# Three-layer kernel on one core: the weights' low words shifted by ScalarE, VectorE's conversion in one pass, and the last block stored in another order

## The chip, the core and the metric

The kernel runs on 1 core of a Trainium2 chip. The metric is the device time of one execution in microseconds. The kernel before takes 1051.12 us (median of 3 runs, 1050.27 to 1051.77). Names of engines: PE is TensorE's matmul, PEld its weight load, DVE is VectorE, ACT is ScalarE, POOL is GpSimd, SP is SyncE, which issues all DMAs here.

## The reference

Three steps follow one another. Tokens are 2304 = 4 x 576, the model width is 512.

```
attention(q, k, v)          # (4, 8, 576, 64): softmax over 4x pooled keys, repeated 4 times,
                            # plus softmax over a band |i - j| < 4
x  = attention as (2304, 512)
h  = x @ w_in               # 512 -> 2048
x  = (max(h, 0) + alpha * min(h, 0)) @ w_out          # 2048 -> 512
xn = x / sqrt(mean(x*x) + 1e-6) * rms_g
g  = xn @ w_gate            # 512 -> 1536
y  = (g * sigmoid(g) * (xn @ w_val)) @ w_out2         # 1536 -> 512
```

All inputs are 64-bit floats in DRAM, and the output is 32-bit.

## The kernel before

**Conversion of the weights.** Every weight matrix comes as pairs of 32-bit words, and the kernel makes 32-bit floats of them itself. A matrix is cut into pieces (`Piece`, L976): w_in and w_out six each, w_gate, w_val and the second w_out four each. A piece is loaded in two halves (`load`, L985) into a raw tile `wr` of 128 x 768 pairs (two halves per matrix of the first layer have 128 x 256). `decode` (L1014) works on one half with three instructions: ACT scales the high words in place (L1018), DVE shifts them left by three into the result `wc` (L1020), and DVE shifts the low words right by 29 and ORs them in (L1021). Then ACT squares the piece with a running sum (L1031), TensorE sums over the partitions (`allps`, L319), DVE makes a power of two from it, and `split` (L344) writes the weight as two 16-bit halves, high by ACT (L345) and low by DVE (L346). So a product of two matrices takes three 16-bit matmuls.

**Blocks.** The tokens are taken in 6 blocks of 384. Layer one (`m1`) runs over 16 units of 128 hidden columns: 12 matmuls `hps` (L1248), ACT and DVE for the leaky relu (L1252, L1254) and the split, and 12 matmuls `acc` (L1261) two units later. Layer two (`m2`, L1327) runs over 12 units: 24 matmuls `gps` (L1340) for gate and value, ACT's tanh (L1349), two passes of DVE (L1351, L1354), the split into `uhl` (L1356, L1357), and 9 matmuls `oacc` (L1365) two units later. At the end of a block three groups of 128 tokens are moved out of PSUM by ACT (L1395) and stored (L1407). Attention of later blocks (`local_tasks`, L431: products on DVE and POOL, L447 and L495, sums on DVE, L458 and L508) and the conversion of layer two's weights run as background work beside the matmuls of layer one's first blocks and layer two's first block.

**What sets the order.** All instructions are recorded first, then `issue_order` (L24) puts them in a fixed order on each engine. It plays the program through with a table of costs per instruction (`cost`, L86) and waits per pair of engines, 20 times back and forth, and keeps the best order. Every engine, SP included, works through its list in order, so one waiting instruction holds up all behind it. A change of a few instructions gives other costs and so another order everywhere.

**The end.** The last block's stores have a DRAM side of 4 rows of time steps by 32 chunks by 512 columns (L1405); the earliest block, in the first batch, has one of 128 rows by 512 columns (L1403).

## Time and profile before

| | |
|---|---|
| median of 3 runs | 1051.12 us |
| the profiled execution, its own time | 1050.03 us |
| its span, first to last instruction | 1048.3 us |
| mean granted TensorE clock (1 is 2.4 GHz) | 0.985 |
| PE busy | 972.9 us |
| DVE busy | 710.8 us |
| ACT busy | 474.0 us |

The profile is of one execution. Busy time is a union of an engine's instructions; a group's row gives how many instructions of one line there are, their busy time together and the mean of one, and behind the second bar the idle time of the engine just ahead of them with what ended it. The chain of waits is followed back from the last instruction. A wait's row names who waited and for whom, the total, the number of times and the longest.

### The profile page before, as it was taken

The numbers are of one execution on the slowest core, as the hardware profiler recorded it, in microseconds if no ns is written. First come the engines' busy times: TensorE is split into PE (matmuls) and PEld (weight loads), VectorE is DVE, ScalarE is ACT, GpSimd is POOL, SyncE is SP. The second block draws the span as 40 slices with busy tenths as digits, with TensorE's granted clock in tenths as the row PEclk, the third lists the DMA queues.
The fourth block names the chain that finished last, engine by engine and source line by source line (L and its number), as shares of the span: only waits on it lengthen the run. The fifth ranks groups of instructions, "written<-read, shape, count | busy, mean of one in ns | idle before, by whom it ended". The sixth has DMA issues, their size and how long they took to land.

```text
span 1048.3 us, 16289 instructions
## 1 busy us (share of the span) xinstructions
PE 972.9 (93%) x6232; PEld 610.5 (58%) x6232; DVE 710.8 (68%) x1515; ACT 474.0 (45%) x1178; POOL 141.3 (13%) x118
## 2 busy tenths in 40 slices
PE   3598998899999699999999999999999999999995
PEld 2465666668975355555666565555556566555553
DVE  0468988999999986999966599993333353442331
ACT  2896868767965365123366432222232332321211
POOL 2522121101021101333200232310000000000000
PEclk9999989999999899999999999999999999999998
DMA  9974635564322023112122021100010000000000
GB/s 169 187 162 126 189 123 159 183 195 127 116 91 91 29 92 123 48 74 61 41 74 78 22 76 46 31 21 11 1 31 2 1 1 1 1 1 8 23 1 31
DMA packets 49972, 74.54 MB, mean 71 GB/s; under 512 B 17682, under 2 KB 30886, under 8 KB 49894
## 3 DMA queue, kind: packets, MB, share of 16 engines
q1 hardware_dynamic: 49894, 73.50, 25.0%
q8 instruction: 49, 0.80, 0.3%
q14 instruction: 29, 0.24, 0.1%
HBM read 68.76 MB, written 4.72 MB: 70 GB/s over the span
## 4 chain that ended last, share of the span: by engine, by line
PE 63%; DVE 19%; DMA 7%; ACT 5%; issue 3%; SPq 1%; POOL 0%; ACTq 0%; POOLq 0%; DVEq 0%
PE gps L1340 19%; PE acc L1261 14%; PE hps L1248 13%; PE oacc L1365 9%; DMA out_dram<-ob 4%; DVE prod L508 2%; DVE ls L458 2%; DVE prod L447 1%; PE avps L649 1%; DVE w L346 1%; DVE prod L495 1%; DVE wc L1021 1%; PE lsps L837 1%; DVE hps L1254 1%; DVE lo L508 1%
## 5 line engine op out<-in xcount | busy, mean ns | idle before, releaser
L1248 PE MATMUL hps<-xt,wi 128*128 128x192 f16 (+1 forms) x1536 | 345.5, 292 | 5.7 <-DVE ghl L346 3.4
L1340 PE MATMUL gps<-x,w 128*128 128x384 f16 x1728 | 343.8, 327 | 4.1 <-DVE th L1351 2.8
L1261 PE MATMUL acc<-ghl,wo 128*128 128x384 f16 (+1 forms) x960 | 247.3, 310 | 0.4 <-ACT ob L1395 0.4
L1340 PEld LDWEIGHTS <-w 128*128 128x128 f16 x1728 | 169.8, 99 | 119.5 <-issue 8.2
L1365 PE MATMUL oacc<-w,uhl 128*128 128x512 f16 x648 | 195.1, 379 | 2.1 <-ACT ob L1395 1.7
L1248 PEld LDWEIGHTS <-wi 128*128 128x128 f16 x1536 | 148.1, 100 | 64.3 <-issue 12.9
L1261 PEld LDWEIGHTS <-wo 128*128 128x128 f16 x1344 | 129.1, 99 | 68.6 <-issue 5.8
L1254 DVE SCALAR_TENSOR_TENSOR hps<-g,oma,hps 128x192 f32<-128x192 f32 (+1 forms) x128 | 65.9, 516 | 77.9 <-ACT g L1252 77.6
L1349 ACT ACTIVATE th<-gps,tsc 128x384 f32<-128x384 f32 x72 | 41.8, 580 | 141.6 <-PE gps L1340 141.3
L1351 DVE SCALAR_TENSOR_TENSOR th<-th,gps 128x384 f32<-128x384 f32 x72 | 39.5, 549 | 97.7 <-ACT th L1349 97.6
L1365 PEld LDWEIGHTS <-uhl 128*128 128x128 f16 x648 | 63.5, 98 | 69.8 <-issue 3.2
L1252 ACT ACTIVATE g<-hps 128x384 f32<-128x384 f32 x96 | 47.0, 490 | 107.3 <-PE hps L1248 106.8
L1356 ACT ACTIVATE uhl<-gps 128x384 f16<-128x384 f32 x72 | 35.3, 490 | 111.0 <-DVE gps L1354 99.6
L447 POOL TENSOR_TENSOR prod<-cq,ckv 128x896 f32<-128x896 f32 x24 | 51.0, 2124 | 240.1 <-PE avps L649 72.6
L1261 PE MATMUL acc<-g,wo 128*128 128x384 f16 (+1 forms) x384 | 67.4, 286 | 2.3 <-DVE wo L346 1.4
L495 POOL TENSOR_TENSOR prod<-ls,ckv 128x896 f32<-128x896 f32 x24 | 44.1, 1837 | 185.0 <-DVE lo L508 97.2
L508 DVE TENSOR_TENSOR prod<-prod 128x384 f32<-128x384 f32 (+1 forms) x108 | 63.3, 596 | 2.3 <-POOL prod L495 2.3
L345 ACT ACTIVATE ghl<-hps,sc 128x384 f16<-128x384 f32 x72 | 41.8, 582 | 50.2 <-DVE hps L1254 44.3
L346 DVE SCALAR_TENSOR_TENSOR ghl<-hps,sc,ghl 128x384 f16<-128x384 f32 x72 | 44.1, 614 | 23.6 <-ACT ghl L345 23.3
L458 DVE TENSOR_REDUCE ls<-prod 128x14 f32<-128x896 f32 x54 | 57.7, 1075 | 0.0
L1357 DVE TENSOR_TENSOR uhl<-gps,uhl 128x384 f16<-128x384 f32 x72 | 39.7, 552 | 22.3 <-ACT uhl L1356 22.2
L1354 DVE SCALAR_TENSOR_TENSOR gps<-th,kap,gps 128x384 f32<-128x384 f32 x60 | 37.1, 618 | 10.6 <-PE gps L1340 7.5
(229 smaller groups left out, 1213.2 us busy)
## 6 DMA issues: line engine op xcount, KB each, us to landing
wr<-in_moe_w_out_dram SPq DMA_DIRECT2D x18, 512.0 KB
wr<-in_moe_w_in_dram SPq DMA_DIRECT2D x20, 384.0 KB
wr<-in_moe_w_gate_dram SPq DMA_DIRECT2D x8, 768.0 KB
wr<-in_moe_w_val_dram SPq DMA_DIRECT2D x8, 768.0 KB
ckv<-in_k_dram SPq DMA_DIRECT2D x7, 768.0 KB
ckv<-in_v_dram SPq DMA_DIRECT2D x7, 768.0 KB
wr<-in_moe_w_out_dram SPq DMA_DIRECT2D x20, 256.0 KB
out_dram<-ob SPq DMA_DIRECT2D x13, 256.0 KB
```

The lines of the kernel that those rows point to most:

```text
L345: nc.scalar.activation(out=hi, in_=src, func=AF.Copy, scale=s)
L346: nc.vector.scalar_tensor_tensor(out=lo, in0=src, scalar=s, in1=hi, op0=ALU.mult, op1=ALU.subtract)
L447: engs[i].tensor_tensor(out=pr, in0=view(st["q"][:, j, t:t + TP], [[D, TP], [0, ND], [1, D]]), in1=view(st["k"][:, j, t:t + TP], [[D, TP], ...
L458: nc.vector.tensor_reduce(out=st["s"][:, j, t:t + TP], in_=st.pop(("p", i)), axis=AX.X, op=ALU.add)
L495: engs[i].tensor_tensor(out=pr, in0=view(st["s"][:, j, t:t + TP], [[ND, TP], [1, ND], [0, D]]), in1=view(st["v"][:, j, t:t + TP], [[D, TP] ...
L508: add = lambda o, a, c: nc.vector.tensor_tensor(out=o, in0=a, in1=c, op=ALU.add)
L1248: nc.tensor.matmul(ps[:, j], wi[:, f + j, a, kk * 128:(kk + 1) * 128], x[:, b_, kk, c0:c0 + n], start=(i == 0), stop=(i == 3 * KK - 1))
L1252: nc.scalar.activation(out=g, in_=ps, func=AF.Relu, scale=-1.0)
L1254: nc.vector.scalar_tensor_tensor(out=ps[:, j], in0=g[:, j], scalar=oma[:, f + j:f + j + 1], in1=ps[:, j], op0=ALU.mult, op1=ALU.add)
L1261: nc.tensor.matmul(acc[e], wo_f(f)[:, a, e * 128:(e + 1) * 128], hl[:, b_], start=(f == 0 and i == 0), stop=(f == NF - 1 and i == 2))
L1340: nc.tensor.matmul(ps, w2_t[i0 + f // 3].rearrange("p a (k c) -> p a k c", k=KK)[:, a, kk, (f % 3) * 128:(f % 3 + 1) * 128], xh[:, b_, kk] ...
L1365: nc.tensor.matmul(acc[tt], t[:, a, tt * 128:(tt + 1) * 128], w[:, b_, f % 3], start=(f in first and i == 0), stop=(f in last and i == 2))
```

## The change

The conversion of all matrices but w_in is altered: ACT takes a second pass, on the low words, as an unsigned number times 2^-29, less a little over one half, through Relu, into an integer (which leaves the top three bits); DVE then shifts the high words and ORs in ACT's result in one pass. A constant column `nhalf` is added. In the last block of layer two, the `uhl` tiles are written with the tokens in another order; the last two units' `oacc` matmuls are recorded group by group; each group of 128 tokens leaves PSUM in two halves of 256 columns, one by ACT and one by DVE; and its store has a DRAM side of 32 chunks by 4 rows by 512 columns.

```diff
--- before.py
+++ after.py
@@ -289,6 +289,7 @@
 
     ident = const.tile([128, 128], F32, name="ident")
     ones = const.tile([128, 1], F32, name="ones")
+    nhalf = const.tile([128, 1], F32, name="nhalf")
     maskp = const.tile([128, 2, W, ND], F32, name="maskp")
     edge = const.tile([128, 3], F32, name="edge")
     pidx = edge[:, 2:3].bitcast(I32)
@@ -351,6 +352,7 @@
             out=ident, in_=ident, pattern=[[-1, 128]], compare_op=ALU.is_equal, fill=0.0, base=0, channel_multiplier=1
         )
         nc.vector.memset(ones, 1.0)
+        nc.vector.memset(nhalf, -0.5 - 2.0 ** -20)
         nc.gpsimd.iota(pidx, pattern=[[0, 1]], base=0, channel_multiplier=1)
         nc.vector.tensor_scalar(out=pidx, in0=pidx, scalar1=NC - 1, scalar2=None, op0=ALU.bitwise_and)
         nc.vector.tensor_scalar(out=edge[:, 0:1], in0=pidx, scalar1=0, scalar2=NEG, op0=ALU.is_equal, op1=ALU.mult)
@@ -1017,6 +1019,12 @@
             hi, lo = r[:, :, :, 1], r[:, :, :, 0]
             nc.scalar.activation(out=hi.bitcast(F32), in_=hi.bitcast(F32), func=AF.Prelu, scale=2.0 ** -112,
                                  alpha=2.0 ** 32)
+            if self.w is not w_in:
+                nc.scalar.activation(out=lo, in_=lo.bitcast(mybir.dt.uint32), func=AF.Relu, scale=2.0 ** -29,
+                                     bias=nhalf)
+                nc.vector.scalar_tensor_tensor(out=d, in0=hi, scalar=3, in1=lo,
+                                               op0=ALU.logical_shift_left, op1=ALU.bitwise_or)
+                return
             nc.vector.tensor_scalar(out=d, in0=hi, scalar1=3, scalar2=None, op0=ALU.logical_shift_left)
             nc.vector.scalar_tensor_tensor(out=d, in0=lo, scalar=29, in1=d,
                                            op0=ALU.logical_shift_right, op1=ALU.bitwise_or)
@@ -1353,8 +1361,12 @@
             kp = 2.0 ** -P_U if m == 0 else kap[:, f // 3:f // 3 + 1]
             nc.vector.scalar_tensor_tensor(out=vp, in0=u, scalar=kp, in1=vp, op0=ALU.mult, op1=ALU.mult)
             t = hl_p.tile([128, 2, BW], F16, tag="hl", name="uhl")
-            nc.scalar.activation(out=t[:, 0], in_=vp, func=AF.Copy)
-            nc.vector.tensor_tensor(out=t[:, 1], in0=vp, in1=t[:, 0], op=ALU.subtract)
+            t0, t1 = t[:, 0], t[:, 1]
+            if m == NBLK - 1:
+                vp = vp.rearrange("p (x t c) -> p x t c", x=NT, c=NC)
+                t0, t1 = [x.rearrange("p (x c t) -> p x t c", x=NT, c=NC) for x in (t0, t1)]
+            nc.scalar.activation(out=t0, in_=vp, func=AF.Copy)
+            nc.vector.tensor_tensor(out=t1, in0=vp, in1=t0, op=ALU.subtract)
             uhl[f] = t
 
         def o_part(f):
@@ -1375,20 +1387,46 @@
                     if f < NF2 - 1:
                         acc[tt] = ps_a.tile([128, DM], F32, tag=f"a{tt}", name=f"oacc{tt}")
 
+        def o_last():
+            for tt in range(NT):
+                for f in range(NF2 - LA, NF2):
+                    w = w2_t[8 + f // 3].rearrange("p a (f e) -> p a f e", f=3)
+                    for i, (a, b_) in enumerate(((0, 0), (0, 1), (1, 0))):
+                        nc.tensor.matmul(acc[tt], uhl[f][:, a, tt * 128:(tt + 1) * 128], w[:, b_, f % 3],
+                                         start=False, stop=(f == NF2 - 1 and i == 2))
+
+        def store_last(tt):
+            o = raw_p.tile([128, DM], F32, tag="raw", name="ob")
+            HD = DM // 2
+            nc.scalar.activation(out=o[:, 0:HD], in_=acc[tt][:, 0:HD], func=AF.Copy, scale=col(INV2))
+            nc.vector.tensor_scalar(out=o[:, HD:DM], in0=acc[tt][:, HD:DM], scalar1=col(INV2), scalar2=None,
+                                    op0=ALU.mult)
+            TQ = 128 // NC
+            b, t = divmod(m * 2 * T + tt * TQ, TT)
+            assert t + TQ <= TT and b > 0
+            nc.sync.dma_start(out=bass.AP(tensor=out.tensor, offset=out.offset + (b * S + t) * DM,
+                                          ap=[[TT * DM, NC], [DM, TQ], [1, DM]]), in_=o)
+
         first, last = (range(0, NF2, 3), range(2, NF2, 3)) if m == 0 else ((0,), (NF2 - 1,))
         if m == 0:
             part = xt_p.tile([128, NT, DM], F32, tag="xt", name="part")
 
+        ends = m == NBLK - 1
         for f in range(NF2 + LA):
             if f < NF2:
                 h_part(f)
-            if f >= LA:
+            if f >= LA and not (ends and f >= NF2):
                 o_part(f - LA)
             if f < NF2:
                 slot(f, NF2)
+        if ends:
+            o_last()
         for tt in range(NT):
             if m == 0:
                 o = part[:, tt]
+            elif ends:
+                store_last(tt)
+                continue
             else:
                 tag = "raw" if m == NBLK - 1 else "ob"
                 o = pool_of(tag).tile([128, DM], F32, tag=tag, name="ob")
```

The order of all engines is made anew. On DVE, at the conversion of layer two's last piece, the kernel before has these rows (`wc_4032` is that piece, `wr_4033` and `wr_4042` its two raw halves, `prod`, `lo` and `ckv_3956` belong to the attention of the third block; the numbers count tiles in order of recording):

```order
L1020 TENSOR_SCALAR wc_4032<-wr_4033 128x768
L508 TENSOR_TENSOR lo_4038<-prod_4036 128x2x64
L1021 SCALAR_TENSOR_TENSOR wc_4032<-wr_4033,wc_4032 128x768
L508 TENSOR_TENSOR prod_4045<-prod_4045 128x2x192
L495 TENSOR_TENSOR prod_4053<-ls_3872,ckv_3956 128x896
L508 TENSOR_TENSOR prod_4045<-prod_4045 128x2x2x64
L1020 TENSOR_SCALAR wc_4032<-wr_4042 128x768
L508 TENSOR_TENSOR lo_4038<-prod_4045 128x2x64
L1021 SCALAR_TENSOR_TENSOR wc_4032<-wr_4042,wc_4032 128x768
```

The same place in the changed kernel, where all tile numbers here are higher by two and L1025 is the new single pass:

```order
L1025 SCALAR_TENSOR_TENSOR wc_4034<-wr_4035 128x768
L1136 TENSOR_SCALAR gsc_121<-rg_103,sw2_118 128x4
L510 TENSOR_TENSOR prod_4047<-prod_4047 128x2x2x64
L497 TENSOR_TENSOR prod_4055<-ls_3874,ckv_3958 128x896
L510 TENSOR_TENSOR lo_4040<-prod_4047 128x2x64
L1025 SCALAR_TENSOR_TENSOR wc_4034<-wr_4044 128x768
```

Four instructions of this piece have become two, and the piece stands 30 rows earlier in DVE's list (616 and 621, from 647 to 655).

On ACT, around the same piece's high words, the kernel before has:

```order
L1356 ACTIVATE uhl_3930<-gps_3916 128x384
L1018 ACTIVATE wr_4033<-wr_4033 128x768
L1349 ACTIVATE th_3999<-gps_3986,tsc_119 128x384
L1018 ACTIVATE wr_4042<-wr_4042 128x768
L345 ACTIVATE w2_3975<-wc_3886,gsc_120 128x384 x4
```

The changed kernel has there (`uhl` and `th` belong to the matmuls of layer two's first block):

```order
L346 ACTIVATE xt_3777<-xs_3773,sc_104 128x4x96
L1020 ACTIVATE wr_4044<-wr_4044 128x768
L1023 ACTIVATE wr_4044<-wr_4044,nhalf_99 128x768
L1357 ACTIVATE th_3813<-gps_3800,tsc_120 128x384
L1020 ACTIVATE wr_4035<-wr_4035 128x768
L1368 ACTIVATE uhl_3830<-gps_3816 128x384
L1023 ACTIVATE wr_4035<-wr_4035,nhalf_99 128x768
```

Two instructions became four, and they stand in front of the tanh of an earlier unit (`th_3813`, where the kernel before has `th_3999`).

## Rows read from the trace of the kernel before

**Rows 1.** The page: busy time, share of the span and instructions of each engine.

```profile
PE 972.9 (93%) x6232; PEld 610.5 (58%) x6232; DVE 710.8 (68%) x1515; ACT 474.0 (45%) x1178; POOL 141.3 (13%) x118
```

**Rows 2.** Windows by stage: stretch, length, busy time (instructions) per engine, clock, DMA.

```profile
core 0: us, PE busy (x) PEld busy (x) DVE busy (x) ACT busy (x) POOL busy (x), PEclk, DMA share, GB/s
...
100.00:195.00 95.00, 82.98 (x617) 59.96 (x617) 85.49 (x203) 74.97 (x224) 16.21 (x11) 0.93 0.51 156
195.00:300.00 105.00, 102.84 (x1027) 87.76 (x1026) 101.53 (x239) 80.16 (x166) 11.26 (x6) 1.00 0.45 141
300.00:340.00 40.00, 38.76 (x246) 23.83 (x245) 38.70 (x84) 23.10 (x47) 7.48 (x4) 1.00 0.30 98
340.00:360.00 20.00, 11.56 (x55) 6.50 (x54) 20.00 (x48) 6.37 (x14) 4.43 (x2) 0.74 0.09 30
360.00:700.00 340.00, 334.66 (x2005) 193.76 (x2004) 290.57 (x575) 132.63 (x346) 70.13 (x38) 1.00 0.19 60
```

**Rows 3.** Timeline of PE from 342 us: start, length, line, [idle before <- releaser].

```profile
342.30 2.93 PE L1340 MATMUL gps<-x,w 128*128 128x384 f16 x17
350.39 0.59 PE L319 MATMUL allps<-s,ones 128*128 128x3 f32 x2 [5.16 <-ACT sqs L1031]
...
355.15 0.45 PE L529 MATMUL xps<-ident,lo 128*128 128x128 f32 x1 [2.38 <-DVE xs L542]
```

**Rows 4.** Waits of PE, 100 to 360 us: total us, times, longest.

```profile
PE allps L319 <- ACT sqs L1031: 6.8, 2, 5.2
...
PE hps L1248 <- DVE g L346: 2.2, 3, 1.7
```

**Rows 5.** Groups, 95 to 357 us: shape, count | busy us, mean ns | idle before.

```profile
L1018 ACT ACTIVATE wr<-wr 128x768 f32<-128x768 f32 x34 | 30.8, 907 | 0.7 <-DMA wr<-in_moe_w_gate_dram 0.7
...
L1021 DVE SCALAR_TENSOR_TENSOR wc<-wr,wc 128x768 int32<-128x768 int32 x24 | 24.5, 1022 | 0.0
...
L1020 DVE TENSOR_SCALAR wc<-wr 128x768 int32<-128x768 int32 x24 | 13.4, 559 | 0.0
...
L1020 DVE TENSOR_SCALAR wo<-wr 128x768 int32<-128x768 int32 x10 | 7.0, 699 | 0.0
```

**Rows 6.** Groups of the whole span, three ACT rows and a DVE row.

```profile
L1349 ACT ACTIVATE th<-gps,tsc 128x384 f32<-128x384 f32 x72 | 41.8, 580 | 141.6 <-PE gps L1340 141.3
...
L1356 ACT ACTIVATE uhl<-gps 128x384 f16<-128x384 f32 x72 | 35.3, 490 | 111.0 <-DVE gps L1354 99.6 <-DVE sc L933 5.3 <-PE oacc L1365 3.6
...
L1395 ACT ACTIVATE ob<-oacc,sc 128x512 f32<-128x512 f32 x15 | 10.3, 686 | 24.1 <-DMA out_dram<-ob 16.1 <-PE oacc L1365 8.0
...
L1254 DVE SCALAR_TENSOR_TENSOR hps<-g,oma,hps 128x192 f32<-128x192 f32 x64 | 26.3, 414 | 5.4 <-ACT g L1252 5.3
```

**Rows 7.** Waits of the DMA-issuing queue, 300 to 390 us.

```profile
SPq L411 <- DVE prod L447: 19.8, 1, 19.8
```

**Rows 8.** Chain of waits: start us, us, what.

```profile
895.65 5.85 PE gps L1340 x36
...
1032.01 5.84 PE oacc L1365 x27
```

**Rows 9.** Timeline of the end.

```profile
1036.05 3.13 SPq L1407 DMA_DIRECT2D out_dram<-ob  x3
...
1037.93 0.69 ACT L1395 ACTIVATE ob<-oacc,sc 128x512 f32<-128x512 f32 x1 [0.67 <-PE oacc L1365]
```

**Rows 10.** Waits of the DMA-issuing queue, 1030 us to the end.

```profile
SPq L1566 <- DMA out_dram<-ob: 8.1, 1, 8.1
```

**Rows 11.** Chain of waits, an earlier store.

```profile
772.15 5.82 DMA out_dram<-ob
```

**Rows 12.** Windows: silence behind a store, a store of block 0, the last stores.

```profile
402.40:403.40 1.00, 1.00 (x7) 0.36 (x5) 0.80 (x3) 0.61 (x2) 0.00 (x0) 1.00 1.06 377
...
695.50:696.50 1.00, 1.00 (x8) 0.56 (x7) 1.00 (x3) 0.00 (x0) 0.15 (x1) 1.00 0.00 0
...
1038.60:1046.60 8.00, 0.00 (x0) 0.00 (x0) 0.00 (x0) 0.02 (x1) 0.00 (x0) 0.68 0.25 92
```

## The prediction

> **What bounds the kernel now.** I read the page first, then windows by stage, then PE's waits and its timeline where it idles, then the groups of the conversion, and last the end of the program. PE is busy for 972.9 of 1048.3 us [rows 1]; the reader is to see that a gain must come from the 75 us in which PE does not work. The windows show where these lie [rows 2]. From 360 to 700 us PE idles 5.3 us in 340, though DVE is 85% busy, so that stage is PE's. The other places are the first 195 us, one hole at 340 to 360 us, and the end.
>
> In the hole PE is busy for 11.56 of 20 us, at a mean granted clock of 0.74 against 1.00 around it, so part of it ran at 1.2 GHz after the idle time, and DVE is busy for all 20 [rows 2]. A gate product takes 5.85 / 36 = 0.1625 us at full clock [rows 8], so the 55 products in the hole are worth 8.9 us, and 11.1 us are lost. The timeline names the wait: PE has nothing from 345.2 us (342.30 + 2.93) until the squares of layer two's last weight piece come at 350.4, and waits again for DVE's attention sums [rows 3]. These squares wait for DVE's conversion. The last piece's load is late as well: SP's list holds it behind a load of the third block's attention, which waits 19.8 us for DVE's products [rows 7]. From 100 to 340 us DVE is busy for 85.49 + 101.53 + 38.70 = 225.7 of 240 us, ACT for 74.97 + 80.16 + 23.10 = 178.2 [rows 2]. So the hole is set by DVE's list.
>
> **The change part by part.** *DVE loses a pass.* 24 passes of 0.559 us and 10 of 0.699 us go, 13.4 + 7.0 = 20.4 us, and two of a third of the width, 0.4 us more: 20.8 us [rows 5]. All stand ahead of the last weight. The pass that stays reads two strided streams instead of one strided and one dense. The nearest row is the pass as it is, 1.022 us [rows 5]; I take no change for it. If the second strided stream halved the rate it would cost about 0.8 us x 34 = 27 us more, if it shed some of today's contention a tenth of a microsecond less, 3 us.
>
> *ACT gets a pass.* The pass on the high words takes 0.907 us [rows 5]; the new one has a column as a bias. A row with a column operand takes 580 ns where one without takes 490 [rows 6], so I take 0.907 + 0.09 = 1.0 us, and 34 and two thirds of them make 34.6 us. No row shows ACT reading unsigned integers: from below 0.907 (31 us in all), from above double, 62 us. The place of 34.6 us is ACT's idle time, 240 - 178.2 = 61.8 us between 100 and 340 us; ACT goes from 74% to 89% busy there. What it delays stands behind it in the list: in the order shown, the tanh of a unit of layer two now stands behind two passes that must wait for the last load. I charge 2 us to PE for such delays, with bounds 0 and 13.8 (the whole of ACT's surplus, 34.6 - 20.8).
>
> *What this gives in the hole.* The last weights come up to 20.8 us earlier by DVE's list, and the load in front of them too, since its DVE products move up in the list with the rest. PE does not come 20.8 us earlier: it is 97.7% busy from 195 to 340 us (102.84 + 38.76 of 145). So the hole closes and little more: -11 us. From one side it could stay as it is, 0; from the other, all of it and the rest of DVE's 20.8 us.
>
> *What it gives before the hole.* Ahead of layer one's second product PE waits 2.2 us for the split by DVE and 6.8 - 5.2 = 1.6 us for the squares of w_out [rows 4], and w_out's passes on DVE go too. Of these 3.8 us I take 2; the bounds are -6 and +6, since every engine's order from the first microsecond on is a new one.
>
> *After the hole* all goes to PE's time, and a shift of PE is a shift of the end. DVE's attention work up to 700 us, 290.6 us in 340 [rows 2], moves up with it.
>
> *The end.* PE's last product ends at 1032.01 + 5.84 = 1037.85 us [rows 8]. Now ACT moves 512 columns in 0.69 us, the three stores' issues end at 1036.05 + 3.13 = 1039.18 [rows 9], the queue then waits 8.1 us for the last landing [rows 10], to 1047.3, and 1.0 us is left to the span's end. During that wait the DMA share is 0.25 at 92 GB/s [rows 12]: a quarter of the 16 engines, with all three stores in line on the same four. By the share a store is 8.0 x 0.25 / 3 = 0.67 us of 16 engines' time, or 2.7 us on four. A store that ran alone landed after 5.82 us [rows 11], of which 2.7 are the four engines', so 3.1 are fixed; the first microsecond behind such an issue shows no traffic [rows 12]. On 16 engines that is 3.1 + 0.7 = 3.8 us; in the microsecond in which a store of block 0 ran among loads, the share was 1.06 and the rate 377 GB/s [rows 12], which leaves room for less, and I take 3.4 us. Moving 256 columns by ACT takes about 0.69 - 256 x 0.00082 = 0.48 us, with 0.82 ns a column from 686 ns for 512 and 580 for 384, all with a column operand [rows 6]; DVE takes 192 columns out of PSUM in 414 ns [rows 6], so its 256 take about as long, beside ACT. The span then ends at 1037.93 + 0.48 + 0.03 + 3.4 + 1.0 = 1042.8 us, 5.5 us earlier. Bounds: -4.9 (3.8 us, and a slower DVE half) and -6.3.
>
> What the row shows is that a store over 4 time steps goes to a quarter of the engines; that 32 chunks would go to all is not in a row. The Trainium skill (DMA: Bandwidth & Descriptors, Why a DMA increments its semaphore by 16 and not by 1) says that a transfer uses the largest number up to 16 that divides the slowest dimension of both sides, which gives 4 before and 16 now; by it the term above stands, and the trace agrees for the 4.
>
> The last block's `uhl` is written 8 bytes apart by ACT and DVE, 24 instructions. PE has 27 products lined up at 1032.01 [rows 8] and needs the last unit's tile only in the latter part of them; I charge 0.2 us, with bounds 0 and 0.6.
>
> *Sum.* -11 - 2 + 2 - 5.5 + 0.2 = -16.3 us from the profiled execution's 1050.03, so 1033.7. The median of the runs stands 1.1 us above that execution: 1034.8 us.
>
> **The rivals.** *Only the end gains.* ACT takes DVE's place or a load does, and the hole stays with its 11 us. For it: the last load's wait behind attention and ACT's 89%. Against it: DVE is busy without a break in the hole, ACT for 6.37 of 20 us. 1051.1 - 5.3 = 1045.8 us.
>
> *All of DVE's time comes back*, as PE's idle 12.0 us from 100 to 195 us close too: 1051.1 - 20.8 - 5.3 = 1025.0 us. Against it, PE's 97.7%.
>
> *Slower: ACT sets the last weights.* Place: ACT's list from 100 to 340 us. If its in-order waits stay as they are and none of the 61.8 idle us takes the new passes, the last piece comes 34.6 - 20.8 = 13.8 us later, the hole grows by as much, and the time is 1051.1 + 13.8 - 5.3 = 1059.6 us. It decides from the point at which the last weights come more than 5.3 us later than now. For it: the new pass is dearer (1.0 us) than the one that it replaces (0.56 to 0.70). Against it: 61.8 us of idle time. The Trainium skill (ScalarE: Activation LUTs, Rules for kernel authors) advises VectorE and not ScalarE for a relu; that would make this rival the case, and what the trace shows against it is that here DVE and not ACT is the engine without idle time.
>
> *The store does not do what it says*, staying on four engines, while the middle gains: 1034.8 + 5.1 = 1039.9 us.
>
> **How the numbers follow.** Forecast 0.50 (its own range 1029 to 1041), only the end 0.20, all of DVE's time 0.14, ACT 0.08, the store on four engines 0.08. The range is 1025 to 1047 us; outside it lie the slower case and part of the unknown costs. About 0.2% (2.1 us) can be told from no change. The forecast, the full gain and the store's case are faster, 0.72; of the 0.20 nearly all, less a mishap of 3 us in the new order, makes 0.89. No change 0.04, slower 0.07.
>
> **What would show it.** DVE's conversion rows: 34 fewer long passes and the OR pass near 1.02 us. ACT: 34 new rows near 1.0 us. The hole between layer two's first products and its last weights: PE idle under 4 us, granted clock near 1.00. The end: the queue's last wait near 3 us, DMA share well above 0.25. I am wrong if PE waits for ACT's squares as long as now, if the OR pass takes 1.8 us, or if the span's last product ends after 1037.85 us.

## The result and the profile after

The changed kernel takes 1037.14 us in the median of 4 runs (1034.70 to 1040.75), the kernel before, run beside it, 1050.92 (1050.27 to 1051.77): a ratio of 0.987, 95% interval 0.984 to 0.990. The forecast was 1034.8 us, its own range 1029 to 1041. Six more runs of the changed kernel gave 1037.38 (f4 below). One kernel's runs differ by some 5 us, in f2 below by 15, and the granted clock goes along: of those six the fastest, 1035.86 us, had 0.990 in the mean and the slowest, 1041.24, 0.978; 21 further runs of the kernel before lie between 1048.38 and 1058.52 us. Ahead of 200 us TensorE is at 1.2 GHz for stretches that differ from run to run: from 160 to 200 us the mean granted clock is 0.96 in the profile of the changed kernel and 0.81 in that of f1, which has the same instructions in the same order there. So small differences are read from profiles below, place by place, and not from medians.

The windows of the profiled execution, with the columns of [rows 2] (the header stands again):

```profile
core 0: us, PE busy (x) PEld busy (x) DVE busy (x) ACT busy (x) POOL busy (x), PEclk, DMA share, GB/s
100.00:195.00 95.00, 90.54 (x641) 64.99 (x642) 79.48 (x187) 82.75 (x231) 16.16 (x11) 0.91 0.46 146
195.00:300.00 105.00, 96.42 (x969) 83.01 (x968) 100.05 (x218) 93.30 (x182) 17.63 (x8) 0.98 0.48 155
300.00:340.00 40.00, 40.00 (x262) 25.35 (x261) 37.48 (x97) 28.67 (x59) 3.63 (x2) 1.00 0.24 80
340.00:360.00 20.00, 18.86 (x110) 10.73 (x108) 18.87 (x42) 7.85 (x15) 2.74 (x1) 1.00 0.14 40
360.00:700.00 340.00, 335.62 (x2015) 194.50 (x2014) 288.08 (x581) 132.49 (x349) 72.07 (x38) 1.00 0.19 60
```

The hole at 340 to 360 us is gone: 110 products where there were 55, at a granted clock of 1.00 where it was 0.74 [rows 2]. From 195 to 300 us something was lost: PE's 102.84 us became 96.42, and ACT went from 80.16 to 93.30. The groups of the conversion, 80 to 360 us, answer to [rows 5]; the waits of PE, 100 to 360 us, to [rows 4]:

```profile
L1023 ACT ACTIVATE wr<-wr,nhalf 128x768 int32<-128x768 uint32 x34 | 34.0, 1000 | 0.0
...
L1020 ACT ACTIVATE wr<-wr 128x768 f32<-128x768 f32 x34 | 30.8, 907 | 0.0
...
L1025 DVE SCALAR_TENSOR_TENSOR wc<-wr 128x768 int32<-128x768 int32 x24 | 25.8, 1077 | 1.5 <-ACT wr L1023 1.5
...
L1025 DVE SCALAR_TENSOR_TENSOR wo<-wr 128x768 int32<-128x768 int32 x10 | 10.2, 1024 | 3.8 <-ACT wr L1023 3.7
```

```profile
PE hps L1256 <- DVE g L347: 2.8, 4, 1.3
PE acc L1269 <- ACT ghl L346: 2.7, 1, 2.7
PE allps L320 <- ACT sqs L1039: 2.7, 2, 1.5
```

The two-input pass hardly got slower (1022 to 1077 ns for layer two's pieces), the new ACT pass takes the 1.0 us that was charged for it, and DVE now waits for ACT ahead of 5 of its passes, 1.5 + 3.7 us. PE's wait for the squares fell from 6.8 to 2.7 us.

The end, by the timelines of ACT, DVE and the DMA-issuing queue and by that queue's last wait, answers to [rows 9, 10]:

```profile
1028.66 0.47 ACT L1401 ACTIVATE ob<-oacc,sc 128x256 f32<-128x256 f32 x1 [0.88 <-PE oacc L1395]
```

```profile
1029.17 0.48 DVE L1402 TENSOR_SCALAR ob<-oacc,sc 128x256 f32<-128x256 f32 x1 [0.87 <-ACT ob L1401]
```

```profile
1026.88 3.34 SPq L1407 DMA_DIRECT2D out_dram<-ob  x3
```

```profile
SPq L1604 <- DMA out_dram<-ob: 1.8, 1, 1.8
```

The last wait is 1.8 us instead of 8.1. The two halves of an eviction do not run side by side: in all three, the DVE half starts when the ACT half has ended, and is released by it. Half a microsecond of the last store, by windows, answers to [rows 12]; 16 engines are at work, not four:

```profile
1031.00:1031.50 0.50, 0.00 (x0) 0.00 (x0) 0.00 (x0) 0.00 (x0) 0.00 (x0) 1.00 1.02 385
```

A first division of the time starts from the moment at which PE starts the sum of the last layer-two weight piece's squares (`allps`), since no layer-two work can be complete ahead of it. The first row is the changed kernel's, from its timeline of PE; in the kernel before the row starts at 350.39 and the second of its two sums at 350.6 [rows 3].

```profile
344.06 0.28 PE L320 MATMUL allps<-s,ones 128*128 128x3 f32 x2
```

Worked out from the traces of all kernels run, in us: that moment (W); what VectorE did and did not do until then (the union of its busy intervals, and the rest); PE's idle time from its first second-product of layer one to its first product of layer two (I); the time from W to the start of the last product of layer two's second block; from there to the end of the last product of all; the tail to the span's end.

| kernel | W | DVE busy, idle | I | W to block 2 | to last product | tail |
|---|---|---|---|---|---|---|
| before | 350.6 | 286.5, 64.1 | 2.2 | 127.0 | 560.2 | 10.5 |
| after | 344.1 | 273.8, 70.3 | 8.6 | 124.2 | 560.3 | 4.4 |
| f4, after again | 346.4 | 271.9, 74.5 | 8.2 | 124.2 | 560.7 | 4.4 |
| e1, end only | 356.0 | 283.9, 72.1 | 2.2 | 127.6 | 560.7 | 4.4 |
| e2, conversion only | 347.1 | 274.6, 72.6 | 8.8 | 124.3 | 560.0 | 10.5 |
| e3, w_out and end | 361.2 | 290.8, 70.4 | 1.7 | 126.9 | 561.3 | 4.4 |
| e4, layer two and end | 349.1 | 280.9, 68.3 | 5.0 | 125.0 | 559.3 | 4.4 |
| f1, x permuted | 351.6 | 273.8, 77.8 | 7.9 | 124.3 | 560.0 | 4.2 |
| f2, prices raised | 344.1 | 273.8, 70.3 | 6.4 | 124.7 | 561.7 | 4.4 |
| f3, half of layer two | 360.0 | 277.9, 82.1 | 2.0 | 128.4 | 561.1 | 4.4 |
| g1, f1 and f2 | 339.2 | 272.3, 66.8 | 6.5 | 124.4 | 561.8 | 4.2 |
| g2, interval prices | 353.2 | 274.9, 78.3 | 2.9 | 123.6 | 557.4 | 4.2 |
| g3, short squares | 342.4 | 279.5, 63.0 | 3.2 | 128.1 | 561.1 | 4.4 |
| h1, short attention | 339.3 | 262.0, 77.3 | 0.8 | 123.5 | 555.9 | 4.4 |

Behind W every kernel takes nearly the same: 124 to 128 us to the second block's end (the upper values where a hole is left), then some 560. So the change is -6.5 us in W, -2.8 in the part with the hole, -6.1 in the tail: -15.3 us between the two spans. Until W, VectorE does 12.7 us less work and idles 6.2 us more.

This divides the time, and two things limit what it says of the cause. The first is that W is the weights' time in the kernel before, where PE waits 5.16 us for the squares [rows 3], but not in the changed one. In the changed kernel their last instruction on ACT ends 1.2 us ahead of W, and PE does not idle at all from layer two's first product, at 297.4 us, to W:

```profile
342.15 0.63 ACT L1039 ACTIVATE sqs<-wc 128x512 bf16<-128x512 f32 x1
342.69 0.19 ACT L1039 ACTIVATION_READ_ACCUMULATOR sqs<-wc 128x1 f32 x1
```

The weights come in time there, and W is the place of `allps` in PE's own list. The second is scatter. Ahead of the last block e1 has the lists of the kernel before, and f4, f1 and e2 have those of the changed kernel (DVE, ACT and POOL in the same order, instruction for instruction). So there are two profiles of one order and four of the other, and W alone spreads over 5.4 and 7.5 us in them. Two stretches of PE's hardly spread (all in us):

| kernel | first second-product of layer one at | from it to layer two's first product | from that to block 2's last product |
|---|---|---|---|
| before | 194.4 | 100.4 | 182.8 |
| e1 | 200.0 | 100.2 | 183.5 |
| after | 185.7 | 111.7 | 170.9 |
| f4 | 188.1 | 111.3 | 171.2 |
| f1 | 192.6 | 111.3 | 172.0 |
| e2 | 187.0 | 112.0 | 172.5 |

In the mean of these the change brings about -9 us up to the first second-product, +11 in the second stretch, and -11.5 in the third, which holds the hole. With the tail's -6.1 that makes some 15 us, near the 13.8 between the medians. Of the -9 and the +11 some 5 us are only moved: 46 products `hps` of layer one that stood ahead of the first second-product now stand behind it, with 98.3 us of PE busy in the second stretch before and 103.1 after.

### The profile page after: what moved, and what is told of

Its sections match the earlier page's. It is cut to its first block, busy times and chain, and to the rows that moved or that the text cites. A ratio compares the mean times of both kernels' runs of the same rounds, so it can differ in the third digit from the quotient of the medians.

```text
span 1033.0 us, 16284 instructions
## 1 busy us (share of the span) xinstructions
PE 977.2 (95%) x6232; PEld 611.1 (59%) x6232; DVE 699.2 (68%) x1483; ACT 506.1 (49%) x1214; POOL 142.1 (14%) x118
## 4 chain that ended last, share of the span: by engine, by line
PE 73%; DVE 10%; ACT 8%; DMA 5%; issue 2%; SPq 1%; POOL 0%; ACTq 0%; DVEq 0%
PE gps L1348 24%; PE hps L1256 15%; PE acc L1269 13%; PE oacc L1377 12%; DMA out_dram<-ob 3%; PE avps L651 2%; ACT sqs L1039 1%; PE lops L893 1%; ACT wr L1020 1%; PE sps L612 1%; DVE ls L460 1%; DVE prod L449 1%; DMA wr<-in_moe_w_in_dram 1%; PE lsps L839 1%; ACT wr L1023 1%
## 5 line engine op out<-in xcount | busy, mean ns | idle before, releaser
L1256 PE MATMUL hps<-xt,wi 128*128 128x192 f16 (+1 forms) x1536 | 359.9, 296 | 4.1 <-DVE g L347 2.8
L1269 PE MATMUL acc<-ghl,wo 128*128 128x384 f16 (+1 forms) x960 | 251.6, 311 | 5.4 <-ACT ghl L346 2.7
L1377 PE MATMUL oacc<-w,uhl 128*128 128x512 f16 x630 | 192.9, 379 | 1.4 <-ACT ob L1433 1.4
L1256 PEld LDWEIGHTS <-wi 128*128 128x128 f16 x1536 | 153.5, 103 | 68.0 <-issue 16.4
L1368 ACT ACTIVATE uhl<-gps 128x384 f16<-128x384 f32 x72 | 41.6, 577 | 99.1 <-DVE gps L1362 92.8
L449 POOL TENSOR_TENSOR prod<-cq,ckv 128x896 f32<-128x896 f32 x24 | 52.6, 2194 | 250.3 <-DMA ckv<-in_k_dram 74.2
L1369 DVE TENSOR_TENSOR uhl<-gps,uhl 128x384 f16<-128x384 f32 x72 | 45.3, 629 | 30.6 <-ACT uhl L1368 30.4
L510 DVE TENSOR_TENSOR prod<-prod 128x384 f32<-128x384 f32 (+1 forms) x108 | 59.7, 563 | 5.4 <-POOL prod L497 5.4
L1020 ACT ACTIVATE wr<-wr 128x768 f32<-128x768 f32 (+1 forms) x48 | 41.5, 865 | 1.7 <-DMA wr<-in_moe_w_in_dram 1.7
```

What stands on the lines that cost most here:

```text
L449: engs[i].tensor_tensor(out=pr, in0=view(st["q"][:, j, t:t + TP], [[D, TP], [0, ND], [1, D]]), in1=view(st["k"][:, j, t:t + TP], [[D, TP], ...
L510: add = lambda o, a, c: nc.vector.tensor_tensor(out=o, in0=a, in1=c, op=ALU.add)
L1020: nc.scalar.activation(out=hi.bitcast(F32), in_=hi.bitcast(F32), func=AF.Prelu, scale=2.0 ** -112, alpha=2.0 ** 32)
L1256: nc.tensor.matmul(ps[:, j], wi[:, f + j, a, kk * 128:(kk + 1) * 128], x[:, b_, kk, c0:c0 + n], start=(i == 0), stop=(i == 3 * KK - 1))
L1269: nc.tensor.matmul(acc[e], wo_f(f)[:, a, e * 128:(e + 1) * 128], hl[:, b_], start=(f == 0 and i == 0), stop=(f == NF - 1 and i == 2))
L1369: nc.vector.tensor_tensor(out=t1, in0=vp, in1=t0, op=ALU.subtract)
```

## The experiments

**e1, the end alone.** The conversion is the former one:

```diff
-    nhalf = const.tile([128, 1], F32, name="nhalf")
+    nhalf = None
...
-            if self.w is not w_in:
+            if False:
```

> The last block's part alone (tokens reordered, eviction in halves, stores over 32 chunks), the conversion as before. Theory A (the parts add up, each in its place): the tail from PE's last product to the end falls from 10.5 to about 4.4 us, PE's last product stays at 1037 to 1038.5 us, the time is about 1045 us. Theory B (the new order, not the conversion's engines, made the gain ahead of the end): the order is made anew here too, so PE's last product would move by several us although no conversion is changed.

1044.75 us (1043.51 to 1050.56), ratio 0.994 (0.991 to 0.997): the end alone gives some 6 us. The tail shows it without scatter, 4.4 us against 10.5. The hole is as it was. The profile is of one of the slowest runs, 1050.45 us, and so its last product ends at 1044.3 us and not at 1037 to 1038.5; the delay is ahead of the first second-product, where the order is that of the kernel before.

**e2, the conversion alone.** The end is the former one:

```diff
-            if m == NBLK - 1:
+            if False:
...
-        ends = m == NBLK - 1
+        ends = False
```

> The conversion alone, the last block as before. Theory A: PE reaches layer one's second product near 186 us, layer two's first product near 297, and ends near 1028; tail 10.4 us; the time is about 1043 us. Theory B: another new order, so the milestones scatter by several us from those of the changed kernel.

1042.29 us (1039.18 to 1044.73), ratio 0.990 (0.987 to 0.994). The two parts add: 5.9 and 8.3 us off the common 1050.62 make 14.2, both together gave 13.8.

**e3, of the conversion only w_out's words, and the end.**

```diff
-            if self.w is not w_in:
+            if self.w is w_out:
```

> Only w_out's low words go to ACT, layer two's stay with DVE in two passes. Theory A (layer two's ACT passes cost PE about 11 us between 195 and 300 us, and closing the hole at 340 us gives about as much back): second product near 186 us, layer two's first product 8 us earlier than before (near 287), PE's wait for the last weight piece stays at 5 us or more, time 1036 to 1039 us. Theory B: no such pattern; layer two's first product stays near 297 us.

1052.88 us (1045.23 to 1059.01), ratio 1.001 (0.998 to 1.004): 8 us slower than e1. That was not expected by either theory. W comes at 361.2 us, and the hole is there again, with its clock: the window and the waits of PE from 300 to 400 us show it.

```profile
340.00:360.00 20.00, 13.14 (x68) 7.90 (x67) 20.00 (x45) 9.80 (x22) 4.89 (x3) 0.83 0.37 118
```

```profile
PE gps L1348 <- DVE uhl L1369: 6.0, 1, 6.0
PE allps L320 <- ACT sqs L1039: 3.1, 1, 3.1
```

VectorE was busy for 290.8 us until W, 6.9 more than in e1, although it has twelve passes fewer to do. Its list does not hold more: ahead of the last weight pass the other instructions are those of e1, group for group and by number, save the writing of `nhalf`. By durations the conversion fell from 74.2 to 70.2 us (that of w_in included), and the same other instructions took 265.1 us instead of 256.3. Why they took longer was not found. PE waits for VectorE as before (6.0 us for a tile of `uhl`). A saving of a few microseconds on the engine that limits can be lost in the order that is made anew.

**e4, of the conversion only layer two's words, and the end.**

```diff
-            if self.w is not w_in:
+            if self.w is not w_in and self.w is not w_out:
```

> Only layer two's low words go to ACT. Theory A: second product as before, near 194 us, ACT over 88% busy between 195 and 300 us, layer two's first product near 305 us (11 us later than before), the hole at 340 us closed, time 1042 to 1046 us. Theory B: layer two's first product stays near 295 us and the time is that of the changed kernel or better.

1040.35 us (1039.51 to 1041.62), ratio 0.988 (0.983 to 0.993): 4.4 us faster than e1, with the hole closed (PE 19.14 of 20 us). Layer two's first product starts at 304.4 us, as theory A had it; the time is 2 us below its range, and ACT is 83% busy from 195 to 300 us (87.59 of 105) and not over 88%. Layer two is the part that matters, but e3 and e4 do not add to e2, +8.1 and -4.4 against -8.3.

**f1, the order of the last block's tokens made in x, and one eviction pass.** The permuted write moves from 24 writes of `uhl` to four products ahead of them; ScalarE evicts all 512 columns.

```diff
...
+                if m == NBLK - 1:
+                    xo = x.rearrange("p (x c t) -> p x t c", x=NT, c=NC)
+                    xi, r = [y.rearrange("p (x t c) -> p x t c", x=NT, c=NC) for y in (xi, r)]
+                nc.vector.tensor_tensor(out=xo, in0=xi, in1=r, op=ALU.mult)
...
+            nc.scalar.activation(out=o, in_=acc[tt], func=AF.Copy, scale=col(INV2))
```

> The changed kernel with two edits at its end. The token order that the last block's stores want is made in the four products x = x1*r of that block, and no longer in the 24 writes of uhl; and ScalarE alone evicts all 512 columns of each final tile. TensorE's order is the changed kernel's, row for row. Theory (the writes of uhl take twice as long because they are permuted, 1.03 and 1.01 us in the changed kernel's trace): both fall back to 0.5 us, the four x products cost up to 0.4 us more each, TensorE's waits of 0.5 us for uhl near 1024 us go, and the time between the last layer-two block's start and the last matmul falls by 0.5 to 1.5 us. Rival: the length is in the 16-bit output or in the PSUM source, and the writes stay at 1 us. Eviction: the halves in the changed kernel ran one behind the other (0.47 and 0.48 us), so that one pass of 512 columns (0.69 us) ends 0.25 us sooner; if they had run side by side, it ends 0.2 us later. Whole kernel: 1035 to 1037.

1038.61 us (1033.06 to 1041.80), ratio 0.986 (0.983 to 0.989), above the 1035 to 1037 expected and not to be told from the changed kernel's. The profile can tell what the writes did. First the changed kernel's writes of the last two blocks (duration: least, median, largest), then f1's, then f1's four permuted products:

```profile
L1368 ACT ACTIVATE uhl<-gps x24: 490/756/1031, 890.5 to 1023.2; 128x384 f16<-128x384 f32 x24
L1369 DVE TENSOR_TENSOR uhl<-gps,uhl x24: 558/784/1022, 891.1 to 1024.3; 128x384 f16<-128x384 f32 x24
```

```profile
L1368 ACT ACTIVATE uhl<-gps x24: 482/490/491, 898.2 to 1031.0; 128x384 f16<-128x384 f32 x24
L1369 DVE TENSOR_TENSOR uhl<-gps,uhl x24: 556/558/558, 898.7 to 1031.5; 128x384 f16<-128x384 f32 x24
```

```profile
L1234 DVE TENSOR_TENSOR ra<-x,rps 128x384 f32<-128x384 f32 x4 | 3.3, 858 | 0.1
```

So it is the 8-byte stride of the writes, and neither the type nor the PSUM source, that doubles them. What PE paid for it is hardly more than the scatter: from the fifth block's first gate product to the last product f1 takes 144.4 us, the changed kernel 144.7 and, in f4, 145.1; but f2 and g1, which differ by the same edit, take 144.8 both. So it is between 0 and 0.7 us. One pass of 0.69 us shortens the tail from 4.42 to 4.19 us, as the halves one behind the other (0.47 + 0.48) would have it.

**f2, the planner's prices of the weight passes raised** to the durations of the groups:

```diff
+        if ins and ins[0].tensor.name.startswith("wr"):
+            if e == "Activation":
+                return 1000 * n / 768
+            return (1050 if len([a for a in ins if free(a) > 1]) > 1 else 560) * n / 768
```

> The changed kernel with the planner's price of the weight passes set near what the trace shows: 1000 ns for 768 columns on ScalarE (it counted 733 for the scaling pass and 826 for the new one), 1050 ns for the merging pass and 560 for the one-input pass on VectorE. The instructions are the same and only their order moves. Theory (the 11 us given back between 195 and 297 us come from ScalarE passes that the planner placed ahead of the layer-one activations because it thought them shorter than they are): the first product of layer two starts 3 to 8 us sooner than the changed kernel's 297.4, and the kernel takes 1029 to 1034. Rival (ScalarE and VectorE are simply full there, whatever the order): the start stays within 2 us of 297, and the kernel takes 1035 to 1039.

1034.95 us (1031.03 to 1046.47), ratio 0.984 (0.979 to 0.988). Layer two's first product starts at 299.1 us, not 3 to 8 us sooner: there the expectation failed. I falls from 8.6 to 6.4 us only, and ACT is as busy as in the changed kernel, 93.78 us from 195 to 300. The order matters by some 2 us there; the load stays.

**f3, ScalarE's pass in w_out and in the second half of each layer-two piece only.**

```diff
-            if self.w is not w_in:
+            if self.w is w_out or (self.w is not w_in and half == 1):
```

> The changed kernel with the new ScalarE pass in w_out and only the second half of every layer-two weight piece; the first halves are converted by VectorE in two passes as before. ScalarE loses 12 passes of 1.0 us, VectorE gains 12 of about 0.56 us. Theory (ScalarE's load is what gives the lead back between 195 and 297 us): the first product of layer two starts 3 to 6 us sooner than 297.4, a part of the hole at 340 to 360 us comes back (2 to 4 us), and the kernel takes 1034 to 1037. Rival (VectorE, busy 100 of 105 us there, is what limits it): the first product of layer two starts at 297 or later, the hole opens as well, and the kernel takes 1039 to 1044.

1055.24 us (1048.41 to 1061.47), ratio 1.002 (0.999 to 1.004): 18 us more than the changed kernel beside it, far outside both expectations. I falls to 2.0 us with ACT's 87.18 us from 195 to 300 us, but layer two's first product starts at 303.4 us, not sooner, and the hole is whole again (PE busy for 15.44 us from 340 to 360, and a wait of 4.4 us for the last squares up to 359.8), as the rival had it, though the time is above the rival's range too. VectorE idles 82.1 us until W. Like e3 it is a mixed kernel that is slow elsewhere. It says that I alone does not set the time.

**f4, the changed kernel again.**

> The changed kernel unaltered, for its scatter and a second profile. If the lead at 195 us (8.7 us on the kernel before) and its loss by 297 us belong to the order of the instructions, the second profile has them both within 2 us; if they are the chance of the half-clock stretches ahead of 195 us, they differ by 4 us or more. Time: 1036 to 1039.

1037.38 us (1035.86 to 1041.24), ratio 0.986 (0.983 to 0.989). Its first second-product starts at 188.1 us (185.7 in the first profile), layer two's first product at 299.5 (297.4), and I is 8.2 (8.6). The loss there belongs to the order. How much of the lead ahead of it is chance these two profiles do not settle: f1 and e2 have the same order there and start their first second-product at 192.6 and 187.0 us, so four profiles spread over 6.9 us, beyond the 4 us that the expectation gave for chance.

**g1, f1 and f2 in one kernel.** No edit beside those.

> The two kernels f1 and f2 in one: the permuted order made in the last block's x products, one eviction pass per final tile, and the planner's raised prices of the weight passes. TensorE's order is that of f2, row for row. If the gain of f2 (medians 1034.95 against 1037.38 in the same call) is its order's, this kernel repeats f2's stretches ahead of 350 us within 2 us and takes 0.5 to 1 us less behind them: 1032 to 1035. If f2's gain was the chance of its half-clock stretches, this kernel takes 1036 to 1039 like the changed one.

1033.78 us (1031.32 to 1045.31), ratio 0.986 (0.981 to 0.990), inside the 1032 to 1035 expected of the order. Its stretches do not repeat f2's within 2 us, though: W is 339.2 against 344.1; the part behind W takes 0.4 us less. f2 and g1 have the same order of PE's; of their twelve runs together seven lie below the lowest of the ten runs of the changed kernel (1034.70) and three above the highest (1041.24), at granted clocks of 0.975 to 0.979 against 0.991 to 0.995 for the others. The median of the twelve is 1034 against 1037.4. A gain of 3 us is likely, not settled.

**g2, the prices of ScalarE's two passes set to what one holds the engine, on f1.** The edit holds f1's two edits as well (the order of tokens made in x, one eviction pass), which the expectation does not say; only the prices are shown. From start to start of passes back to back it is 0.8 and 0.9 us; the timeline of ACT in the changed kernel shows how the durations overlap:

```profile
285.23 0.92 ACT L1020 ACTIVATE wr<-wr 128x768 f32<-128x768 f32 x1
286.02 1.03 ACT L1023 ACTIVATE wr<-wr,nhalf 128x768 int32<-128x768 uint32 x1
286.89 0.66 ACT L1039 ACTIVATE sqs<-wc 128x512 bf16<-128x512 f32 x1
```

```diff
+        if e == "Activation" and ins[0].tensor.name.startswith("wr"):
+            return (885 if len(ins) > 1 else 795) * n / 768
```

> The changed kernel with the planner's price of ScalarE's two weight passes set to what one holds the engine, read from start to start of passes that run back to back: 795 ns for the scaling pass (it counted 733) and 885 ns for the new one (826); the durations in the groups, 907 and 1000 ns, overlap the next instruction's start. VectorE's price is left (869 counted, 869 measured). If an exact price is what the planner lacked, this order is at least as good as f2's, whose prices were too high by 0.1 to 0.2 us a pass: 1030 to 1035. If f2 gained because the overcharged passes were spread out, or by the chance of another order, this kernel lands where the changed one does, or worse: 1035 to 1045.

1041.17 us (1036.91 to 1044.11), ratio 0.990 (0.988 to 0.993): worse than f2 with the better prices, so f2 did not gain by exact prices. Behind W it is the best order of the unabridged kernels (123.6 and 557.4 us); ahead of it PE idles 10.5 us between 105 and 205 us, where the changed kernel idles 5.4, at a mean granted clock of 0.83 (the changed kernel 0.91), which is 34 us of the 100 at 1.2 GHz.

**g3, ScalarE relieved.** The sums of squares of all weights take 64 of each 512 columns.

```diff
+                src = src[:, :, 0:16] if self.f0 is None else src[:, 0:64]
+                o = o[:, :, 0:16] if self.f0 is None else o[:, 0:64]
```

> The changed kernel with the sums of squares of all weights taken over an eighth of the columns (64 of each 512), so the weights' scale is not the reference's: ScalarE loses some 0.37 us in each of 52 squares, 19 us ahead of 360 us, and VectorE's work is as it was. Theory (the lead is given back between 195 and 297 us because ScalarE is full there): ScalarE's busy time from 195 to 300 us falls from 93 to 85 or less, TensorE's idle time between its first second-product and its first layer-two product falls from 8.6 to 2 to 4 us, the kernel takes 1029 to 1033. Rival (VectorE, busy 100 of 105 us there, sets the pace): the idle time stays above 6 us and the kernel takes 1035 to 1039.

1040.12 us (1037.72 to 1040.51), ratio 0.988 (0.987 to 0.990). The windows:

```profile
195.00:300.00 105.00, 101.54 (x1040) 88.74 (x1038) 101.22 (x225) 86.61 (x183) 14.65 (x7) 1.00 0.49 157
...
340.00:360.00 20.00, 14.30 (x69) 7.51 (x68) 16.82 (x41) 5.16 (x12) 3.66 (x1) 0.83 0.12 37
```

The theory was right on the spot, I falls to 3.2 us and layer two starts at 289.1 us, 8.3 sooner, and wrong on the time: W moves by 1.7 us only, and PE, early, waits in a new hole. Its waits from 300 to 360 us are mostly for VectorE's attention sums:

```profile
PE xps L531 <- DVE xs L544: 2.7, 1, 2.7
PE xps L531 <- DVE s L1132: 1.9, 1, 1.9
PE allps L320 <- ACT sqs L1041: 1.0, 1, 1.0
```

ScalarE is busy for 252.1 us until W, 22 less than in the changed kernel (274.0), and in this order that bought nothing.

**h1, VectorE relieved:** half of each score sum and one of three additions of the local attention are left out. By durations that takes 17.6 us off VectorE ahead of the last weight pass, nearly what g3 took off ScalarE. But the local attention goes on behind it, and another 38.5 us go between 360 and 700 us (288.08 to 249.62), which g3 has no counterpart for.

```diff
-                nc.vector.tensor_reduce(out=st["s"][:, j, t:t + TP], in_=st.pop(("p", i)), axis=AX.X, op=ALU.add)
+                nc.vector.tensor_reduce(out=st["s"][:, j, t:t + TP], in_=st.pop(("p", i))[:, :, :, 0:D // 2], axis=AX.X, op=ALU.add)
...
-                add(pr[:, :, 0:3], pr[:, :, 0:3], pr[:, :, 3:6])
```

> The changed kernel with a part of the local attention left out on VectorE: the score sums take half of the columns of each product (448 of 896), and the first of the three additions that sum the weighted values is dropped, so the attention's output is not the reference's. VectorE loses some 0.5 us in each of 16 sums and 0.6 us in each of 18 additions between 100 and 360 us, 19 us in all, about as much as the new ScalarE pass took from it; ScalarE's work is as it was. Theory (VectorE's work sets when the last layer-two weights are ready, and the rest of the kernel follows that at a fixed distance): the last weight's sum comes 7 to 14 us sooner than the changed kernel's 344 to 346, and the kernel takes 1024 to 1031. Rival (since the change ScalarE sets it): the last weight's sum moves by under 4 us, and the kernel takes 1033 to 1039. Behind 480 us, where TensorE is busy throughout, nothing of it shows: 560 us from there to the last product, as in all kernels so far.

1024.84 us (1023.48 to 1026.03), ratio 0.974 (0.972 to 0.976), inside the theory's 1024 to 1031. The windows and W:

```profile
195.00:300.00 105.00, 104.25 (x1063) 90.89 (x1062) 100.59 (x228) 94.55 (x187) 19.85 (x9) 1.00 0.55 177
...
360.00:700.00 340.00, 338.73 (x2037) 196.86 (x2036) 249.62 (x512) 132.24 (x345) 69.06 (x36) 1.00 0.19 60
```

```profile
339.27 0.28 PE L320 MATMUL allps<-s,ones 128*128 128x3 f32 x2
```

ACT is busier than in any other kernel from 195 to 300 us, and PE idles least. W comes 4.8 and 7.1 us ahead of the two profiles of the changed kernel, at the lower edge of what was expected; the squares themselves are done at 336.2 us, 6.7 and 9.0 ahead. The last sentence of the expectation was wrong: behind block 2 the time falls from 560 to 556 us, so a third of the gain of 12.3 us comes of the work left out there. From 360 to 700 us PE's idle time goes from 4.4 to 1.3 us: that stage, too, waits now and then for VectorE. Ahead of it, the stretch to layer two's first product takes 102.6 us, 9 less than in the changed kernel, and the next one 168.6.

## Why the prediction was right, and where it was not

- *DVE's list sets the hole, and losing passes there closes it* (-11 us): right, and in the mechanism too. The stretch with the hole takes 11 to 12 us less in each of four profiles, and PE's 11.0 us of idle time in it are 1.4. That this is not the luck of one order shows in the others: wherever all of layer two's words are converted the new way and the work is otherwise whole (after, e4, f2, g1, g2), PE idles at most 1.5 us there; in the three orders where they are not (before, e3, f3) it idles 10 to 14. In g3, where PE comes 8 us earlier and the weights do not, it is 8.7. That VectorE and not ScalarE sets the pace is argued from h1 against g3 and from the waits of g3's new hole; each of the two is one order only, and orders alone, with the same instructions, moved the median from 1033.8 (g1) to 1041.2 us (g2), so h1's 1024.8 lies beyond that spread and g3's 1040.1 inside it. The rival in which ScalarE sets the last weights, the Trainium skill's advice for a relu (ScalarE: Activation LUTs, Rules for kernel authors) on its side, did not come about.
- *Before the hole, -2, and ScalarE's delays, +2*: the sum was nearly right, and that is luck, since neither size was. In the first profiles layer two's first product starts 2.5 us later than before (297.4 against 294.9), where 0 was forecast; with the repeats it is 294.9 and 300.2 before, 297.4 to 303.9 after, so a loss of some 2 us that the scatter nearly hides. It is what the conversion lacks of the forecast: by e2 it gave 8.3 us and not 11. It is made of -9 and +11, or, without the 5 us of products that only moved, of about -4 and +6. The +6 are PE's idle time between the two points (2.2 to 8.6 us), and both g3 (3.2) and h1 (0.8) take it away: ScalarE's load delays PE there, as charged, and VectorE's as much.
- *What DVE loses reaches the end.* The prediction let the hole take 11 of 20.8 us and left open where the rest stays. By durations the conversion on VectorE fell by 19.3 us until W. 12.7 us less busy time came of it, since other work was done sooner or took longer, and 6.2 us went into idle time, of which the passes that wait for ScalarE's new pass make 5.2. So VectorE was relieved and made to wait by the same edit. And once the weights came in time, at 342.9 us for a W of 344.1, more of the same would not have helped at that place, as long as PE came there no earlier.
- *ScalarE's pass, 1.0 us, 34.6 in all*: right as a duration, too much as a load. Passes back to back start 0.8 and 0.9 us apart, so the load is about 30 us, and ACT is busy for 82.75 + 93.30 + 28.67 = 204.7 of 240 us, 85% and not 89%. The Trainium skill says as much (Perfetto Trace Analysis, Optimizing Scalar/DVE Operations): of an instruction's fixed cost the profile shows about twice what holds the engine, since the half in which the writes are acknowledged overlaps the next instruction. The trace agrees on the overlap, 0.79 us from 285.23 to 286.02 for a duration of 0.92; what fills it no run here shows.
- *The OR pass unchanged*: 1.026 us became 1.024 for w_out, and 1.022 became 1.077 for layer two. Right.
- *The end, -5.5*: 6.1 us in the profile, 5.9 by e1's median. Inside it two errors cancel: eviction takes 0.95 us and not 0.48, and from there to the landing it is 2.4 us and not 3.4 (the last DVE half ends at 1029.17 + 0.48 = 1029.65; the issues end at 1026.88 + 3.34 = 1030.22, and 1.8 of waiting makes 1032.0). That 32 chunks go to 16 engines is shown now by a share of 1.02, as the rule of the Trainium skill had it (DMA: Bandwidth & Descriptors, Why a DMA increments its semaphore by 16 and not by 1).
- *The permuted `uhl`, +0.2*: f1, f2 and g1 say 0 to 0.7 us, where 0 to 0.6 was the range. The prediction looked at who waits and did not price the write itself, which doubled.
- *Behind the hole all is PE's*: nearly. The 560 us hold within 2 for every kernel but g2 (557.4) and h1 (555.9).

What stays open: why e3 and f3, which have fewer passes on VectorE than e1, get their last weights later (W 361.2 and 360.0 against 356.0). In e3 the other instructions took longer, in f3 VectorE idled longer. Each has its own order on every engine, and no kernel was run with a fixed one.

## What to carry to other kernels

Find the moment at which the last of a stage's inputs is ready, and write it as busy plus idle time of the engine that makes it; a pass that is moved away counts by how far that sum falls, which here was a third of what was taken off. See too whether the consumer still waits at that moment: once it does not, the bound has moved on. Then leave out an equal amount of work on each of the two busy engines, in the same stage: the one whose relief moves the end is likely the bound, however full the other looks and however much it delays on the spot. Repeat a profile before a difference of a few microseconds is explained: one order of instructions gave 344 and 352 us for the same moment here. Where a planner makes the order anew, half of a good change can be worse than none, so parts are tested but not summed.

## What the hardware showed beside that

- A write of 16-bit words 8 bytes apart took about twice the time of a dense one: 1031 ns for 490 on ScalarE, 1022 for 558 on VectorE, for 384 columns. A write of 4-byte words 16 bytes apart took 858 ns for 548 on VectorE.
- ScalarE's pass over 768 unsigned integers 8 bytes apart, with a column as bias, took 1000 ns; its pass over as many floating-point words 8 bytes apart, without a column, took 907.
- A store of 256 KB on all 16 engines was a burst within 1.5 us, at 385 GB/s in its middle half microsecond; on four of them three such stores ran for 8 us at 92 GB/s [rows 12].
- Two halves of one tile, written by ScalarE and VectorE out of one PSUM tile, ran one behind the other, the second released by the first. Whether the shared output tile or the PSUM tile is the reason was not tried.
